# Pacing the table scatters and interleaving the end of attention in an attention-plus-experts kernel

## The chip, the cores and the metric

The kernel runs on one core of a Trainium2 chip. The metric is the device time of one execution in microseconds (us); the lower the better. Engines are written as in the profile: PE is TensorE (matmuls), PEld its weight loads, DVE is VectorE, ACT is ScalarE, POOL is GpSimd, SP is SyncE, which here only issues DMAs. L432 is line 432 of the kernel before.

## The reference

Pooled attention, and then a mixture of experts of which each token uses one or none:

```
k_p = k.reshape(B, H, Sp, 8, D).mean(axis=3); v_p likewise      # B=8, H=8, S=576, D=64, Sp=72
attn = softmax(q @ k_p^T / sqrt(D));  x = attn @ v_p             # x: 4608 tokens x 512
do_compute = x @ w_skip > 0                                      # the other tokens keep x
logits = x[do_compute] @ w_gate                                  # 8 experts
e = argmax(logits);  gate = softmax(logits)[e]
out = x + gate * (relu(x @ w1[e]) @ w2[e])                       # w1: 512x1024, w2: 1024x512
```

## The kernel before, in words

**Two phases.** The attention works through 36 tiles of 128 tokens in a software pipeline written out by hand (`for t in range(NT)`, L637): in iteration t, PE computes the scores of tile t (L305), DVE finds each head's extreme (`largest`, L312), ACT takes exponentials of tile t-1 (L319), PE transposes tile t-2 (L330, L334), multiplies tile t-4 with the pooled values (L348, L350), and DVE normalises tile t-5 (L365 to L372) and SP stores it to `out`. So x of tile i is made in iteration i + 5, and "tile 32" below means iteration t = 32. The order on PE, ACT and DVE is that of the program text; the order on POOL and SP is the framework's, which puts an instruction where its own estimate has it ready, and which adds the waits that the data needs, by program order.

**Routing.** The tokens' gate logits come out of the value matmul (`l8`). After each of six groups of tiles (`GROUPS = [9, 9, 7, 6, 3, 2]`) `route` works in small DVE steps (L393 to L429), an exp on ACT (L409) and rank matmuls on PE (L413, L415): logits minus the largest (l, which stands in PSUM), the chosen expert, the token's rank in it. That gives `di`, each token's row in a table in DRAM (token number and gate, by expert), and `scatter(j)` (L431) writes the rows of one tile with an indirect DMA from POOL. `pending` holds the scatters not yet issued; each iteration issues up to `SCATTERS` of them (L709). A dropped token has a row number out of bounds and isn't written.

**Near tokens.** After the second group (18 tiles) the first 256 tokens of the first expert are known. `near_tokens` registers two callbacks: `ids` (L457) `NIDS` iterations later reads rows 0 to 255 of the table into SBUF, `gathers` (L461) `NWAIT` iterations later computes their slots on DVE (L462) and gathers their x into `ring[:, 3]` and `ring[:, 4]` (L464). In the last two iterations PE transposes them (`tx`, L492, copied by ACT L494 and subtracted by DVE L495), and after the loop the first expert's two layers for these tokens are computed in 16 steps (`l1`, `l2`: L502 to L504, L517 to L519) beside the last routing and the planning of the expert loop (`slots`). Their results (L523) go back with an indirect store, that of the first 128 at once (L525), that of the second in the loop's POOL stream (L1016). Meanwhile the first unit's tokens are gathered into `ring[:, 0:3]` (L889), and `tx` transposes these too (`follow`, L788), when two steps are left.

**The expert loop.** One block with a stream per engine follows (`experts`). Units of up to three tiles of one expert's tokens are transposed, multiplied (L1088 to L1090, L1103 to L1106), scattered (L1007) and the next ones gathered (L1002), with weights loaded one expert ahead. Every matmul is split in high and low halves, three products for one.

Also on POOL: the sums over pooled values (`pool_v`, L240 to L247, then L282 and L285, which PE needs at each change of batch) and the low halves of the first expert's weights (L560).

Of the kernel before, what the change touches and what calls it, by code (L numbers as in the profile page):

```python
# [26 lines left out]
F32 = mybir.dt.float32  # L27
# [39 lines left out]
WROWS = 4.0  # L67
LEAD = 0.5
NLAST = 2
TWO = 1  # L70
QUARTERS = 288, 320, 352, 384
HALF = 64
BIT = 3
SCATTERS = 3
NIDS = 4
NWAIT = 5
WARM = 3
SLOTS = 3 * (MAXU + 2)
NO_TOKEN = 1 << 20
# [82 lines left out]
def attention(tc, nc, q, k, vm, vr, cf, w1, w2, whi, wlo, out, c, pay, offs, table, load_constants, near, bufs, late, early, fin):  # L162
    with ExitStack() as ctx:
# [27 lines left out]

        side_ps = ps_m.tile([128, 512], F32, name="mps")
        scratch = side_ps[:, 512 - GMAX * 20:]

        def load_k(b, part=0):
            n = 4 * SP * POOL
# [112 lines left out]
        def largest(sc, nm):  # L309

            for i in range(2):
                nc.vector.tensor_reduce(nm[:, i * 4:i * 4 + 4], sc[i].rearrange("p (h k) -> p h k", k=SP),  # L312
                                        axis=AX.X, op=ALU.min)
            yield

        def exped(sc, nm):
# [56 lines left out]
            nc.sync.dma_start(out[t * 128:(t + 1) * 128, :], flat(x))  # L373
            yield

        scatters, pending = [], []
        starts = [sum(GROUPS[:i]) for i in range(len(GROUPS))]

        def route(t0, n):


            last = t0 + n == NT
            m = n if last else GMAX
            room = ap.tile([128, n * 20], F32, name="r_room", bufs=1) if last else scratch
            lp = room[:, 0:n * 9].rearrange("p (j e) -> p j e", e=9)
            l, skip = lp[:, :, 0:NE], lp[:, :, NE]
            r8 = eq = room[:, m * 9:m * 9 + n * NE].rearrange("p (j e) -> p j e", e=NE)
            cm, se, ds = (room[:, m * (17 + i):m * (17 + i) + n] for i in range(3))
            bc = lambda x: x.unsqueeze(2).broadcast_to([128, n, NE])
            new = lambda name, *s, dt=F32: ap.tile([128, GMAX] + list(s), dt, name=name)[:, :n]  # L390
            mx = new("r_mx"); no = new("r_no"); cn = new("r_cn"); oh = new("r_oh", NE, dt=BF16)
            ex = new("r_ex", NE); sn = new("r_sn"); di = new("r_di", dt=I32)
            nc.vector.tensor_reduce(lp, l8s.pop(t0)[:, :n].rearrange("p j h c -> p j c h"), axis=AX.X, op=ALU.add)  # L393
            yield
            nc.vector.tensor_reduce(mx, l, axis=AX.X, op=ALU.max)
            yield
            nc.vector.tensor_scalar(no, skip, 0.0, float(NO_TOKEN), ALU.is_le, ALU.mult)
            yield
            nc.vector.tensor_tensor(l, l, bc(mx), ALU.subtract)
            yield  # L400
            nc.vector.scalar_tensor_tensor(eq, l, 0.0, epos.unsqueeze(1).broadcast_to([128, n, NE]), ALU.is_equal, ALU.mult)
            yield
            nc.vector.tensor_reduce(cm, eq, axis=AX.X, op=ALU.max)
            yield
            nc.vector.tensor_tensor(cn, cm, no, ALU.add)
            yield
            nc.vector.tensor_tensor(oh, eq, bc(cn), ALU.is_equal)
            yield NEXT
            nc.scalar.activation(ex, l, AF.Exp)  # L409

            rk = side_ps[:, 0:(n + 1) * NE].rearrange("p (j e) -> p j e", e=NE)
            for j in range(n):
                nc.tensor.matmul(rk[:, j:], c["ones"], oh[:, j].unsqueeze(1).broadcast_to([128, n + 1 - j, NE]),  # L413
                                 start=(j == 0), stop=False)
            nc.tensor.matmul(rk[:, 0:n], c["lower"], oh, start=False, stop=True)  # L415
            nc.vector.tensor_tensor(r8, rk[:, 0:n], offs.unsqueeze(1).broadcast_to([128, n, NE]), ALU.add)
            nc.vector.tensor_tensor(offs, offs, rk[:, n], ALU.add)
            yield NEXT
            nc.vector.tensor_tensor(r8, r8, oh, ALU.mult)
            yield  # L420
            nc.vector.tensor_reduce(se, ex, axis=AX.X, op=ALU.add)
            yield
            nc.vector.tensor_reduce(ds, r8, axis=AX.X, op=ALU.add)
            yield
            nc.vector.tensor_scalar(sn, se, 1e-9, None, ALU.add)
            yield
            nc.vector.tensor_tensor(di, ds, no, ALU.add)
            yield
            nc.vector.reciprocal(pay[:, t0:t0 + n, 1], sn)  # L429

            def scatter(j):  # L431
                m = nc.gpsimd.indirect_dma_start(table, bass.IndirectOffsetOnAxis(ap=di[:, j:j + 1], axis=0),  # L432
                                                 pay[:, t0 + j, :], None, bounds_check=NE * NTOK - 1, oob_is_err=False)
                for other in scatters:
                    tc.declare_no_dep(m.ins, other, reason="rows of the table are written once")
                scatters.append(m.ins)

            pending.extend(lambda j=j: scatter(j) for j in range(n))
            if t0 + n == EARLY:
                yield from near_tokens()  # L440

        def near_tokens():

            count = offs[:, 0:1]
            less = ap.tile([128, 1], F32, name="less")
            nn = ap.tile([128, 1], F32, name="nn")
            nc.vector.tensor_scalar(nn, count, 256.0, 2.0, ALU.is_ge, ALU.mult)
            yield
            nc.vector.tensor_scalar(less, count, 256.0, float(NO_TOKEN), ALU.is_lt, ALU.mult)
            yield  # L450
            nc.vector.tensor_scalar(near["first"][:, 0:1], nn, 128.0, None, ALU.mult)
            yield
            nc.vector.tensor_scalar(near["jt"][:, 0:1], nn, -1.0, float(JT), ALU.mult, ALU.add)
            yield
            nc.vector.tensor_tensor(near["place"], c["place"], nn, ALU.add)

            def ids():  # L457
                assert not pending
                nc.sync.dma_start(near["ids"], table[0:256, 0:2].rearrange("(s l) t -> l s t", l=128))

            def gathers():  # L461
                nc.vector.tensor_scalar(near["slot"], near["ids"][:, :, 0], less, None, ALU.add)  # L462
                for i in range(2):
                    nc.gpsimd.indirect_dma_start(bufs["ring"][:, 3 + i, 0:D], None, out[0:EARLY * 128],  # L464
                                                 bass.IndirectOffsetOnAxis(ap=near["slot"][:, i:i + 1], axis=0),
                                                 bounds_check=EARLY * 128 - 1, oob_is_err=False)
            later[t + NIDS] = ids
            later[t + NWAIT] = gathers
            yield
# [3 lines left out]
        def tile_steps():  # L473
# [40 lines left out]
            def l2(i, part):  # L514
# [6 lines left out]
                def result():  # L521
                    res = bufs["ring"][:, 3 + i, 0:D]
                    nc.vector.scalar_tensor_tensor(res, ps, near["ids"][:, i, 1:2], res, ALU.mult, ALU.add)  # L523
                    if i == 0:
                        nc.gpsimd.indirect_dma_start(out, bass.IndirectOffsetOnAxis(ap=near["slot"][:, 0:1], axis=0),  # L525
                                                     res, None, bounds_check=NTOK - 1, oob_is_err=False)
                return result if part == 3 else None

            got = [lambda f2=f2, part=part: l1(f2, part) for f2 in range(4) for part in range(2)]
# [107 lines left out]
        for t in range(NT):  # L637
# [60 lines left out]
                vt[1] = load_v(1)  # L698
            if t == 1:
                start_k(2)  # L700
            if t in (FILL, FILL + 4):
                n = (NE * NTOK + 128) * RT // 128 // 17
                nc.gpsimd.memset(init[:, 0:n], NO_TOKEN if t == FILL else 0.0)
# [2 lines left out]
                                      init[:, 0:n].unsqueeze(1).broadcast_to([128, 17, n]))  # L706
            if t >= WSTART:
                next(wgen, None)
            for _ in range(min(SCATTERS, len(pending))):  # L709
                pending.pop(0)()  # L710
            later.pop(t, lambda: None)()
            if t == NT - 4:
                load_weights(range(5))
# [26 lines left out]

        def products(n):

            while steps and len(waiting) < 3 and clock["pe"] < clock["dve"] + n:
                while 4 < len(steps) <= 8 and len(waiting) >= len(steps) - 4:
                    evacuate()
                after = steps.pop(0)()
# [30 lines left out]
        for wait in slots(tc, nc, c, offs, table, near, bufs, out, fin, ap, ps_m):  # L777
            if wait:

                end = clock["dve"] + wait  # L780
                while clock["pe"] < end and steps:
                    clock["dve"] = max(clock["dve"], clock["pe"] - 2.0)
                    products(2.5)
                    evacuations(clock["pe"] - 1.0)
                clock["dve"] = max(clock["dve"], end)
            else:
                side(STEP)
        follow = [lambda: [tx(ring[:, i], i)() for i in range(3)]]  # L788
        assert not routes.gens
        held = [kinds(e, fin["nti"]) for e in (nc.tensor, nc.scalar, nc.vector)]  # L790
        while steps or waiting or follow:
            clock["dve"] = max(clock["dve"], clock["pe"] - 2.0)
            products(2.5)
            if waiting:
                evacuate()
            if follow and len(steps) <= NLAST:
                follow.pop()()
        return held


# [106 lines left out]
def experts(tc, nc, out, w1, w2, whi, wlo, slot, gate, nti, held, near, bufs, ident, psum):  # L907
# [4 lines left out]
    with tc.tile_critical():  # L912
# [67 lines left out]
        with nc.Block(no_gpsimd_drain=True) as blk:  # L980
# [10 lines left out]
            def _(g):  # L991
# [21 lines left out]
                        done(f"gat{i}", 16)  # L1013
                        V(g, f"land{i}")

                scatter(near["slot"][:, 1:2], 4)  # L1016
                gather(3)
                gather(5)
                done("sc1", 16)
                gather(4)  # L1020
                landed()
                more, on = g.alloc_register("more"), g.alloc_register("on")
                g.reg_load(more, nti[0:1, 2 * UNITS:2 * UNITS + 1])
# [267 lines left out]
```

## Time and profile before

| | |
|---|---|
| time, median of 3 runs | 568.61 us (568.09 to 570.25) |
| the profiled execution | 568.01 us, its span 566.2 us |
| mean granted TensorE clock | 0.967 |
| PE / DVE / ACT / POOL busy | 91% / 52% / 43% / 38% of the span |
| attention with its routing, up to PE's first expert matmul | 0 to 220.4 us |
| expert loop | 220.4 to 566.2 us |

Busy time counts instructions that an engine executes. Text in brackets at the end of a timeline row is the engine's idle time just before that instruction and what, by the semaphores, ended it; "issue" means nothing that the profile shows. [...]

### The profile page before, as it was taken

To read this page: it belongs to the slowest core of one execution; us is meant where nothing else is said; L and a number is where in the kernel's file an instruction comes from. 1 tells how busy PE (TensorE), PEld (TensorE's weight loads), DVE (VectorE), ACT (ScalarE), POOL (GpSimd) and SP (SyncE) were. 2 spreads that over 40 slices of the span, in tenths; PEclk is the share of its full clock that TensorE was granted. 3 is DMA by queue.
4 is the path that set the end of the run, shared out by engine and by line. 5 is a ranking of instruction groups with operands and counts; after the bars stand their busy time and mean duration, and the time that the engine had idled before them with its cause. 6 is when DMAs were issued, how large, how long until landed. Compare 5 with 4: busy or idle time off the path is not lost. (4 is left out here: it accounts for less than half of the span.)

```text
span 566.2 us, 10990 instructions
## 1 busy us (share of the span) xinstructions
PE 517.2 (91%) x3346; PEld 466.1 (82%) x3347; DVE 294.6 (52%) x697; ACT 244.9 (43%) x671; POOL 217.3 (38%) x294
## 2 busy tenths in 40 slices
PE   5899986987878887989999999999999999999994
PEld 2799775776767776888889888989989899989893
DVE  4476746866637542235353545222364648465653
ACT  4598766887852101114232333111243436344441
POOL 5754556299842424130333034223242024304042
PEclk9699997999989788999999999999999999999998
DMA  8999894785651121012451325201144537572210
GB/s 294 380 340 370 335 353 159 278 287 175 201 204 66 41 76 37 22 51 75 158 180 45 113 110 182 74 19 53 56 156 151 198 117 256 197 246 75 101 45 7
DMA packets 35799, 88.92 MB, mean 157 GB/s; under 512 B 7213, under 2 KB 9961, under 8 KB 33887
## 3 DMA queue, kind: packets, MB, share of 16 engines
q1 hardware_dynamic: 27648, 73.98, 37.2%
q0 software_dynamic: 8112, 14.47, 7.8%
q8 instruction: 18, 0.29, 0.2%
q14 instruction: 21, 0.17, 0.1%
HBM read 74.37 MB, written 22.85 MB: 172 GB/s over the span
## 5 line engine op out<-in xcount | busy, mean ns | idle before, releaser
L1088 PE MATMUL psl<-xhi,w1hi 128*128 128x256 f32 (+3 forms) x416 | 123.4, 297 | 5.2 <-PEq L918 3.7
L1090 PE MATMUL psl<-xhi,w1lo 128*128 128x256 f32 (+3 forms) x416 | 122.9, 295 | 0.0
L1089 PE MATMUL psl<-xlo,w1hi 128*128 128x256 f32 (+3 forms) x416 | 122.8, 295 | 0.0
L1144 ACT ACTIVATE hhi<-psl 128x256 fp32r<-128x256 f32 (+4 forms) x104 | 41.9, 403 | 157.5 <-ACTq L918 156.1
L1007 POOL DMA_INDIRECT out<-ring,slot x39 | 39.8, 1019 | 178.4 <-POOLq L918 144.4
L1103 PE MATMUL psf<-w2hi,hhi 128*128 128x512 f32 x240 | 94.8, 395 | 0.9 <-PEq L918 0.9
L1104 PE MATMUL psf<-w2lo,hhi 128*128 128x512 f32 x240 | 93.6, 390 | 0.6 <-issue 0.6
L1201 DVE SCALAR_TENSOR_TENSOR hlo<-psl,hhi 128x256 fp32r<-128x256 f32 (+2 forms) x104 | 43.8, 423 | 82.2 <-DVEq L918 77.7
L1088 PEld LDWEIGHTS psl<-xhi,w1hi 128*128 128x128 f32 x416 | 79.8, 192 | 7.0 <-issue 6.5
L1089 PEld LDWEIGHTS psl<-xlo,w1hi 128*128 128x128 f32 x416 | 79.8, 192 | 0.4
L1090 PEld LDWEIGHTS psl<-xhi,w1lo 128*128 128x128 f32 x416 | 79.8, 192 | 0.0
L1106 PE MATMUL psf<-w2hi,hlo 128*128 128x512 f32 x200 | 78.0, 390 | 0.0
L319 ACT ACTIVATE e<-sc,nm 128x72 f32<-128x72 f32 x288 | 65.1, 343 | 4.1 <-DVE nm L312 3.6
L348 PE MATMUL o<-blocks,pT 128*128 128x148 f32 (+1 forms) x304 | 49.9, 301 | 11.1 <-DVE x L372 6.9
L1190 DVE SCALAR_TENSOR_TENSOR ring<-psf,ring 128x512 f32 x25 | 18.7, 750 | 74.2 <-DVEq L918 74.2
L1103 PEld LDWEIGHTS psf<-w2hi,hhi 128*128 128x128 f32 x240 | 45.1, 188 | 9.8 <-issue 1.1
L348 PEld LDWEIGHTS o<-blocks,pT 128*128 128x128 f32 (+1 forms) x304 | 41.2, 184 | 13.8 <-issue 6.4
L1104 PEld LDWEIGHTS psf<-w2lo,hhi 128*128 128x128 f32 x240 | 45.1, 188 | 8.6
L1002 POOL DMA_INDIRECT ring<-out,slot x39 | 44.3, 1135 | 15.2 <-issue 12.4
L312 DVE TENSOR_REDUCE nm<-sc 128x4 f32<-128x288 f32 x72 | 32.2, 453 | 32.1 <-PE sc L305 15.7
L1153 ACT ACTIVATE xhi<-psd 128x512 fp32r<-128x512 f32 x36 | 18.9, 599 | 67.0 <-ACTq L918 67.0
L432 POOL DMA_INDIRECT table<-pay,r_di x36 | 35.4, 984 | 27.5 <-DVE rc L367 12.1
(219 smaller groups left out, 878.6 us busy)
## 6 DMA issues: line engine op xcount, KB each, us to landing
stage<-in_w SPq DMA_DIRECT2D x64, 512.0 KB, 4.0
out<-x SPq DMA_DIRECT2D x36, 256.0 KB
stage<-in_k SPq DMA_DIRECT2D x6, 1152.0 KB
hlo<-in_vm SPq DMA_DIRECT2D x4, 1024.0 KB
hhi<-in_vm SPq DMA_DIRECT2D x4, 1024.0 KB
xlo<-in_q SPq DMA_DIRECT2D x6, 512.0 KB
qt<-in_q SPq DMA_DIRECT2D x6, 512.0 KB
xhi<-in_q SPq DMA_DIRECT2D x5, 512.0 KB
```

The costliest lines, as they stand in the source:

```text
L319: nc.scalar.activation(e[:, h, :], sc[h // 4][:, h % 4 * SP:(h % 4 + 1) * SP], AF.Exp, bias=nm[:, h:h + 1], scale=-1.0)
L348: nc.tensor.matmul(o_[sl, g * 2 * VA:(g + 1) * 2 * VA], pT[:, 2 * a + g, sl], vbd[b % 3][:, 2 * a + g, :], start=(g == 0), stop=False)
L1002: g.indirect_dma_start(ring[:, s % 6, 0:D], None, out, bass.IndirectOffsetOnAxis(ap=slot[:, s:s + 1], axis=0), bounds_check=NTOK - 1, oob_ ...
L1007: g.indirect_dma_start(out, bass.IndirectOffsetOnAxis(ap=offsets, axis=0), ring[:, s % 6, 0:D], None, bounds_check=NTOK - 1, oob_is_err=Fa ...
L1088: t.matmul(ps, whi[0][:, k, w], xhi[:, k, xs], start=(k == 0), stop=False)
L1089: t.matmul(ps, whi[0][:, k, w], xlo[:, k, xs], start=False, stop=False)
L1090: last = t.matmul(ps, wlo[0][:, k, w], xhi[:, k, xs], start=False, stop=(k == 3))
L1103: t.matmul(ps, hhi[:, k, sl], whi[1][:, k, :], start=(k == 0), stop=False)
L1104: last = t.matmul(ps, hhi[:, k, sl], wlo[1][:, k, :], start=False, stop=(short and k == 7))
L1106: last = t.matmul(ps, hlo[:, k, sl], whi[1][:, k, :], start=False, stop=(k == 7))
L1144: a.activation(hhi[:, f, xs], psL[f % 3][:, xs], AF.Relu).then_inc(sem["act"], 1)
L1201: m = v.scalar_tensor_tensor(to[:, f], psL[f % 3][:, cs], 0.0, hhi[:, f, cs].bitcast(F32), ALU.max, ALU.subtract)
```

## The change

- Scatters are issued one per iteration up to iteration 21 (`EARLY + LAG`), two per iteration from there (`SCATTERS` 3 to 2); the first one of an iteration also waits for that iteration's second L312 (`turn`). Those issued after the loop don't wait.
- `NIDS` goes from 4 to 6 and `NWAIT` from 5 to 7, and `ids` asks only that 18 scatters have been issued, not that none is pending.
- `route` writes l to a tile in SBUF and reads the experts' places from a copy in PSUM (`places`); `l` and `ex` have one buffer.
- The last two `l2` steps are kept back, and the first unit's three transposes alternate with them; four matmuls without use (`IDLE`) follow the last transposes.
- The indirect store of the first 128 near tokens moves from L525 into the expert loop's POOL stream, ahead of the gathers.

```
-SCATTERS = 3
-NIDS = 4
-NWAIT = 5
+SCATTERS = 2
+NIDS = 6
+NWAIT = 7
+IDLE = 4
...
+        places = side_ps[:, 512 - GMAX * 20 - NE:512 - GMAX * 20]
...
             for i in range(2):
-                nc.vector.tensor_reduce(nm[:, i * 4:i * 4 + 4], ...)
+                m = nc.vector.tensor_reduce(nm[:, i * 4:i * 4 + 4], ...)
+            turn[0] = m.ins
...
-            nc.vector.tensor_tensor(l, l, bc(mx), ALU.subtract)
+            nc.vector.tensor_tensor(l, lp[:, :, 0:NE], bc(mx), ALU.subtract)
-            nc.vector.scalar_tensor_tensor(eq, l, 0.0, epos.unsqueeze(1)..., ALU.is_equal, ALU.mult)
+            nc.vector.scalar_tensor_tensor(eq, l, 0.0, places.unsqueeze(1)..., ALU.is_equal, ALU.mult)
...
-            def scatter(j):
+            def scatter(j, apart=False):
...
+                if apart:
+                    tc.add_manual_dep(m.ins, turn[0].name, ..., reason="a token tile's turn")
-            pending.extend(lambda j=j: scatter(j) for j in range(n))
+            pending.extend(lambda *a, j=j: scatter(j, *a) for j in range(n))
...
-                assert not pending
+                assert len(scatters) >= EARLY
...
-                    if i == 0:
-                        nc.gpsimd.indirect_dma_start(out, ...near["slot"][:, 0:1]..., res, ...)
...
+            if t == START:
+                nc.vector.tensor_copy(places, epos)
...
-            for _ in range(min(SCATTERS, len(pending))):
-                pending.pop(0)()
+            for i in range(min(1 if t < EARLY + LAG else SCATTERS, len(pending))):
+                pending.pop(0)(i == 0)
...
-            while steps and len(waiting) < 3 and clock["pe"] < clock["dve"] + n:
+            while len(steps) > NLAST and len(waiting) < 3 and clock["pe"] < clock["dve"] + n:
...
-        follow = [lambda: [tx(ring[:, i], i)() for i in range(3)]]
-        while steps or waiting or follow:
+        while len(steps) > NLAST:
             clock["dve"] = max(clock["dve"], clock["pe"] - 2.0)
             products(2.5)
             if waiting:
                 evacuate()
-            if follow and len(steps) <= NLAST:
-                follow.pop()()
+        for i in range(3):
+            low = tx(ring[:, i], i)
+            if i == 2:
+                o = ps_o.tile([128, 2, 512], F32, name="o")
+                for _ in range(IDLE):
+                    nc.tensor.matmul(o[:, 0, :], whi[0][:, 0, 0:128], whi[1][:, 0, :], start=True, stop=True)
+            while waiting:
+                evacuate()
+            low()
+            if steps:
+                after = steps.pop(0)()
+                if after:
+                    waiting.append((0.0, after))
...
-                scatter(near["slot"][:, 1:2], 4)
-                gather(3)
+                for i in range(2):
+                    scatter(near["slot"][:, i:i + 1], 3 + i)
                 gather(5)
-                done("sc1", 16)
-                gather(4)
+                for i in range(2):
+                    done(f"sc{i}", 16)
+                    gather(3 + i)
```

## Rows read from the trace of the kernel before

**Rows 1.** The page, part 1: busy time, share of the span, instructions of PE.

```profile
PE 517.2 (91%) x3346; PEld 466.1 (82%) x3347; DVE 294.6 (52%) x697; ACT 244.9 (43%) x671; POOL 217.3 (38%) x294
```

**Rows 2.** Windows: length, busy PE, PEld, DVE, ACT, POOL (instructions), clock, DMA share, GB/s.

```profile
80.00:95.00 15.00, 8.02 (x46) 7.06 (x45) 6.93 (x17) 6.41 (x23) 13.02 (x16) 0.78 0.46 173
95.00:120.00 25.00, 23.10 (x188) 20.87 (x188) 21.06 (x59) 20.96 (x77) 10.75 (x14) 1.00 0.79 284
125.00:135.00 10.00, 5.93 (x44) 5.13 (x43) 4.38 (x13) 5.89 (x21) 8.12 (x8) 1.00 0.43 153
160.00:170.00 10.00, 6.73 (x41) 5.91 (x42) 3.58 (x10) 5.73 (x20) 3.40 (x5) 0.83 0.46 155
150.00:155.00 5.00, 5.00 (x43) 4.99 (x42) 4.17 (x17) 4.28 (x18) 4.20 (x5) 1.00 1.01 343
...
220.00:225.00 5.00, 4.64 (x26) 4.66 (x27) 0.42 (x1) 0.39 (x1) 4.00 (x7) 0.66 0.21 57
```

**Rows 3.** Timeline of POOL (start, us, line, operation): scatters, and a gather.

```profile
75.57 1.18 POOL L432 DMA_INDIRECT table<-pay,r_di  x1 [0.65 <-DVE rs L365]
...
86.00 0.97 POOL L432 DMA_INDIRECT table<-pay,r_di  x1 [0.30 <-issue]
...
122.57 1.02 POOL L432 DMA_INDIRECT table<-pay,r_di  x1 [0.16 <-DVE nm L312]
...
150.86 1.08 POOL L464 DMA_INDIRECT ring<-out,nslot  x1 [0.30 <-DVE nslot L462]
...
154.73 1.03 POOL L432 DMA_INDIRECT table<-pay,r_di  x1 [0.17 <-DVE l L371]
...
178.73 1.01 POOL L432 DMA_INDIRECT table<-pay,r_di  x1 [12.10 <-DVE rc L367]
```

**Rows 4.** Timelines of DVE, ACT and PE beside the first and the fourth run.

```profile
81.33 0.17 DVE L365 TENSOR_SCALAR rs<-o 128x8 f32<-128x8 f32 x1 [4.03 <-PE sc L305]
...
85.60 0.60 ACT L331 ACTIVATE pT<-pt 128x512 f32<-128x512 f32 x1 [5.47 <-PE sc L305]
...
189.39 0.28 PE L503 MATMUL sc<-xlo,w1hi 128*128 128x256 f32 x1 [0.33 <-issue]
190.10 0.38 PE L504 MATMUL sc<-xhi,w1lo 128*128 128x256 f32 x1 [0.43 <-issue]
...
191.56 0.60 ACT L509 ACTIVATE hhi<-sc 128x512 fp32r<-128x512 f32 x1 [9.88 <-remote]
```

**Rows 5.** Tiles 31 to 35 and the near tokens: timelines, L459's source view, L1007's landing.

```profile
149.46 1.12 DVE L462 TENSOR_SCALAR nslot<-nids,less 128x2 int32<-128x2 f32 x1
...
151.34 0.68 DVE L372 TENSOR_TENSOR x<-o,rc 128x512 f32<-128x512 f32 x1
...
153.81 0.19 DVE L429 RECIPROCAL pay<-r_sn 128x7 f32<-128x7 f32 x1
...
154.55 0.68 DVE L372 TENSOR_TENSOR x<-o,rc 128x512 f32<-128x512 f32 x1
...
167.94 0.68 DVE L372 TENSOR_TENSOR x<-o,rc 128x512 f32<-128x512 f32 x1
...
168.91 0.66 PE L492 MATMUL pt<-cfs,ring 128*128 128x128 f32 x4
...
L459 SPq DMA_DIRECT2D nids<-table x1: 385/385/385, 142.3 to 142.3; - x1
...
DMA to landing us min/median/max: 2.1/2.8/5.6
```

**Rows 6.** Timelines of PE and DVE at the end of the attention phase.

```profile
213.84 0.66 PE L492 MATMUL mps<-cfs,ring 128*128 128x128 f32 x4 [0.97 <-DVE xlo L495]
...
217.27 0.75 DVE L523 SCALAR_TENSOR_TENSOR ring<-sc,nids,ring 128x512 f32<-128x512 f32 x1 [1.41 <-PE sc L519]
...
220.36 0.37 PE L1088 MATMUL psl<-xhi,w1hi 128*128 128x256 f32 x1 [3.13 <-PEq L918]
```

**Rows 7.** Waits of PE, 120 to 150: total us, times, longest.

```profile
PE mps L413 <- ACT r_ex L409: 1.2, 1, 1.2
```

More of the change, by code (lines that the diff above doesn't have):

```diff
@@ L311, in largest @@
             for i in range(2):
-                nc.vector.tensor_reduce(nm[:, i * 4:i * 4 + 4], sc[i].rearrange("p (h k) -> p h k", k=SP),
-                                        axis=AX.X, op=ALU.min)
+                m = nc.vector.tensor_reduce(nm[:, i * 4:i * 4 + 4], sc[i].rearrange("p (h k) -> p h k", k=SP),
+                                            axis=AX.X, op=ALU.min)
+            turn[0] = m.ins
             yield
@@ L374, in normalised @@
             yield
-        scatters, pending = [], []
+        scatters, pending, turn = [], [], [None]
         starts = [sum(GROUPS[:i]) for i in range(len(GROUPS))]
@@ L385, in route @@
             lp = room[:, 0:n * 9].rearrange("p (j e) -> p j e", e=9)
-            l, skip = lp[:, :, 0:NE], lp[:, :, NE]
+            skip = lp[:, :, NE]
             r8 = eq = room[:, m * 9:m * 9 + n * NE].rearrange("p (j e) -> p j e", e=NE)
@@ L389, in route @@
             bc = lambda x: x.unsqueeze(2).broadcast_to([128, n, NE])
-            new = lambda name, *s, dt=F32: ap.tile([128, GMAX] + list(s), dt, name=name)[:, :n]
+            new = lambda name, *s, dt=F32, **kw: ap.tile([128, GMAX] + list(s), dt, name=name, **kw)[:, :n]
             mx = new("r_mx"); no = new("r_no"); cn = new("r_cn"); oh = new("r_oh", NE, dt=BF16)
-            ex = new("r_ex", NE); sn = new("r_sn"); di = new("r_di", dt=I32)
+            l = new("r_l", NE, bufs=1); ex = new("r_ex", NE, bufs=1); sn = new("r_sn"); di = new("r_di", dt=I32)
             nc.vector.tensor_reduce(lp, l8s.pop(t0)[:, :n].rearrange("p j h c -> p j c h"), axis=AX.X, op=ALU.add)
             yield
-            nc.vector.tensor_reduce(mx, l, axis=AX.X, op=ALU.max)
+            nc.vector.tensor_reduce(mx, lp[:, :, 0:NE], axis=AX.X, op=ALU.max)
             yield
@@ L398, in route @@
             yield
-            nc.vector.tensor_tensor(l, l, bc(mx), ALU.subtract)
+            nc.vector.tensor_tensor(l, lp[:, :, 0:NE], bc(mx), ALU.subtract)
             yield
-            nc.vector.scalar_tensor_tensor(eq, l, 0.0, epos.unsqueeze(1).broadcast_to([128, n, NE]), ALU.is_equal, ALU.mult)
+            nc.vector.scalar_tensor_tensor(eq, l, 0.0, places.unsqueeze(1).broadcast_to([128, n, NE]), ALU.is_equal, ALU.mult)
             yield
@@ L436, in scatter @@
                 scatters.append(m.ins)
-            pending.extend(lambda j=j: scatter(j) for j in range(n))
+                if apart:
+                    tc.add_manual_dep(m.ins, turn[0].name, mybir.DependencyInfo(
+                        mybir.DependencyClass.Sync, mybir.DependencyReason.DATA), reason="a token tile's turn")
+            pending.extend(lambda *a, j=j: scatter(j, *a) for j in range(n))
             if t0 + n == EARLY:
@@ L523, in result @@
                     nc.vector.scalar_tensor_tensor(res, ps, near["ids"][:, i, 1:2], res, ALU.mult, ALU.add)
-                    if i == 0:
-                        nc.gpsimd.indirect_dma_start(out, bass.IndirectOffsetOnAxis(ap=near["slot"][:, 0:1], axis=0),
-                                                     res, None, bounds_check=NTOK - 1, oob_is_err=False)
                 return result if part == 3 else None
@@ L780, in attention @@
                 end = clock["dve"] + wait
-                while clock["pe"] < end and steps:
+                while clock["pe"] < end and len(steps) > NLAST:
                     clock["dve"] = max(clock["dve"], clock["pe"] - 2.0)
```

## The prediction

> **What bounds the kernel now.** I read the page first [rows 1]: PE is busy 91% of the span, so time can only be won where PE stands still or runs at its lower clock. The windows view then shows where that is [rows 2]. The expert loop behind 225 us leaves little. The attention part (up to 180 us) has undisturbed stretches such as 95 to 120, where PE is busy 23.10 of 25 us (0.924), and three bad ones: 80 to 95 with 8.02 of 15 us busy at a mean granted clock of 0.78, 125 to 135 with 5.93 of 10, and 160 to 170 with 6.73 of 10 at 0.83. The timeline of POOL [rows 3] shows what these share. Each lies in the second half of, or just behind, a run of table scatters (L432), which POOL issues every 1.3 us without a pause: 9 from 75.57 on (the last at 86.00), 9 from 122.57, 7 from 154.73 and 9 from 178.73. Rows of a group become ready together, POOL has nothing else to do, and so "three per tile" in the program text has become all of them at once.
>
> The timelines of the other engines [rows 4] say what happens there: everything stands still, not one engine. DVE starts L365 at 81.33 after 4.03 us of idleness, ACT starts L331 at 85.60 after 5.47 us although its transposes on PE were long issued, ACT stands 9.88 us before L509 at 191.56, and there PE itself takes 0.71 us from one matmul of 256 columns to the next (189.39 to 190.10), with no wait in the program between them. The fourth run has almost no other DMA traffic beside it and stalls as well, so a full DMA queue is not needed. The first scatters of a run seem to do no harm: ACT's idle time begins at 85.60 - 5.47 = 80.1, four scatters into the run (DVE's at 77.3, but that one may begin as a regular wait for PE). Two gathers of the same kind in a row at 150.86 [rows 3] stand in a window in which PE is busy 5.00 of 5.00 us [rows 2]. So the stall looks like a matter of density, and the change goes at density.
>
> **The change part by part.** All sums are against the profiled execution's 568.01 us (span 566.2); the median of the three runs is 0.6 higher.
>
> *Pacing.* The first group's 9 scatters go one per tile, those of groups two and three two per tile, the first of a tile waiting for that tile's second L312 on DVE. A tile takes 3.21 us undisturbed (151.34 to 154.55) [rows 5], so POOL then issues 1.3 or 2.6 us in it and pauses. What is to be had: in each bad window, work at full clock is busy time times granted clock, and at the undisturbed 0.924 it would take 8.02 x 0.78 / 0.924 = 6.8 us instead of 15 (8.2 won), 5.93 / 0.924 = 6.4 instead of 10 (3.6 won), 6.73 x 0.83 / 0.924 = 6.0 instead of 10 (4.0 won). Sum 15.8 us [rows 2]. Bounds: 0, if the stall belongs to each scatter however it stands, and 15.8. I take 15.8, by the nearest row, the harmless pair at 150.86. The fourth run (groups four to six, behind the loop) is not paced: there the scatters are issued without the wait, and its stall stays.
>
> *What waits behind the new wait.* POOL is in order; a scatter that waits for a tile's L312 holds back what stands behind it, the value sums (L240 to L242), the low weight halves (L560) and the products L282 and L285 that PE needs at a change of batch. Value sums had been done early. Each change of batch can find POOL one scatter (1.3 us) late; three such changes lie in the paced stretch, some slack covers part: cost 1.0 us, bounds 0 and 4.
>
> *The near tokens' chain* is where I expect a loss. The read of the first 256 table rows (L459) moves from 4 to 6 tiles behind group two, the gathers from 5 to 7. Group two's last route step is in tile 26, so the read comes in tile 32, and group three's rows become ready in that same tile (L429 at 153.81, while the next tile's x is at 154.55) [rows 5]. In the text two of its scatters are issued ahead of the read. They write the table, the read reads it, so it waits for both. Before, the read was issued at 142.3, with all 18 scatters done and group three's not begun [rows 5]. From E = 153.81: POOL issues the first scatter 0.9 us later (154.73) [rows 3], the second 1.3 on, E + 2.2. Landing of an indirect store is 2.1, 2.8 or 5.6 us (min, median, max of L1007's row) [rows 5]. I use it for each hop: second scatter landed E + 5.0, read landed E + 7.8, DVE's L462 to POOL's gather 1.4 us (149.46 to 150.86) [rows 3, 5], gather landed E + 12.0. PE wants it for the transposes L492 in tile 34: x of that tile at 154.55 + 3.21, and 0.97 us on as in tile 35 (167.94 to 168.91) [rows 5], E + 4.9. PE, in order, would stand 7.1 us; with the fastest landings 5.0, with the slowest 15.5. Below that it could be nothing, if the tiles around it are slower than 3.21 us. I take 7.1: the DMA share in 150 to 155 is 1.01 [rows 2], which speaks against the minimum, and the maximum would have to strike three times. Before, this slack was two tiles longer, so the stall is new.
>
> [...]
>
> *Logits on chip.* l goes to its own SBUF tile, a copy of epos into PSUM (one DVE instruction, 0.2 us, in tile 5, hidden beside PE). The rank matmuls L413 no longer share a bank's tile with what ACT's exp L409 reads: 1.2 us of PE's wait for r_ex in 120 to 150 goes [rows 7]. The DVE steps keep their size; nothing else moves.
>
> *The end.* Before, three transposes of the first unit stand in a row and the third waits 0.97 us for DVE (213.84), then two l2 steps, DVE's L523 from 217.27 to 218.02, PE's first expert matmul at 220.36 after 3.13 us idle [rows 6]. After, transposes and steps alternate, which hides the 0.97; but behind the last transposes now stand ACT's copy (0.60, as L331 of the same size [rows 4]) and DVE's subtraction (0.68, as L372 [rows 5]) where L523 (0.75) stood: 0.97 - (0.60 + 0.68 - 0.75) = 0.4 us. The four idle matmuls (0.28 us or more each [rows 4]) lie in a gap in which PE waits anyway. In 220 to 225 PE runs at a granted clock of 0.66 [rows 2], which costs 5 x 0.34 = 1.7 us; a shorter gap may or may not keep the clock, so I count half, 0.8. Bounds of both together 0 and 2.1; taken 1.2. The early store that moves into the loops (L525) was off the path, and the gather of slot 3 comes one scatter later, 1.3 us, with most of a unit in hand: 0.
>
> **Sum.** 15.8 + 1.2 + 1.2 - 7.1 - 1.0 = 10.1; 568.0 - 10.1 = 557.9, and 0.6 for the median: **558.5 us**.
>
> **The rivals.**
> (a) *The chain is hidden.* If landings are quick or the tiles around 32 to 34 slower than 3.21 us, the 7.1 is not paid: 551.4 us. For it: route steps make some tiles longer. Against it: the read is ordered behind scatters that become ready in its own tile.
> (b) *The pacing does not spread.* It is done by a wait, and a POOL that is behind (eight instructions of value sums in a row) finds the waits passed and issues several tiles' scatters together again. Only the first group's stretch would be won, 3.6 + 4.0 lost again: 566.1 us.
> (c) *Nothing happens*: neither stall nor chain moves, the end and L413 give 2.4: 566.2 us.
> (d) *Slower.* The stall is a price of each scatter, 15.8 / 25 = 0.63 us wherever it stands. Then pacing returns nothing and the chain is paid: 568.6 - 2.4 + 7.1 + 1.0 = 574.3 us. It becomes slower than before as soon as less than 5.7 / 15.8, some 36%, of the stall comes back. For it: DVE's idle time begins early in its run [rows 4]. Against it: the harmless first scatters. [...]
>
> **How the numbers follow.** Forecast 0.45 (its own range 554 to 563), (a) 0.22, (b) 0.13, (c) 0.07, (d) 0.13. The range from 550.0 to 568.5 takes in (a) to (c) and leaves out (d) and the best of (a). A measurement of this kernel can tell 0.5% (2.8 us) from no change; (b) lies about on that line and is halved. Faster 0.73, same 0.14, slower 0.13.
>
> **What would show it.** Right: single scatters some 3.5 us apart from 75 us on, then pairs; no idle time of 4 us or more on ACT and DVE before the loop's end; x of tile 28 some 12 us earlier; the stall before L509 still there; PE idle for several us before its first L492, released by a gather. Wrong: stalls of DVE and ACT beside single scatters (d), runs of four or more scatters (b), L492 without a wait (a), or a PE that waits for POOL's L282.

## The result, and the profile after

The change makes the kernel slower: median 574.32 us (573.13 to 575.14) against 568.99 us for the kernel before, ratio 1.0073, 95% interval 1.0049 to 1.0098. The forecast was 558.5. The profiled execution took 573.13 us, its span 571.3.

Where x of a token tile is made (start of DVE's L372, now L375) tells where the time goes; us from the start of the span:

| tile | before | after | difference |
|---|---|---|---|
| 12 | 75.79 | 75.52 | -0.27 |
| 15 | 95.57 | 86.84 | -8.73 |
| 20 | 117.42 | 117.03 | -0.38 |
| 23 | 133.19 | 132.06 | -1.13 |
| 28 | 154.55 | 153.97 | -0.58 |
| 30 | 167.94 | 174.53 | +6.58 |
| 33 | 185.44 | 191.62 | +6.19 |
| first expert matmul | 220.36 | 226.51 | +6.15 |
| end of the span | 566.2 | 571.3 | +5.1 |

8.7 us are won by tile 15 and lost again by tile 20; another 7.2 are lost between tiles 28 and 30. The windows of after show the places (columns as in [rows 2]; the clock is the granted share of the full one, in these rows between 0.50 and 1.00):

```profile
80.00:95.00 15.00, 12.16 (x96) 11.46 (x95) 14.23 (x30) 12.47 (x44) 10.08 (x14) 1.00 0.89 329
...
105.00:115.00 10.00, 5.13 (x39) 4.58 (x38) 9.24 (x13) 4.29 (x18) 9.69 (x13) 0.86 0.28 90
...
125.00:130.00 5.00, 2.98 (x23) 2.58 (x21) 1.66 (x5) 0.73 (x4) 4.08 (x5) 1.00 0.58 219
130.00:135.00 5.00, 3.24 (x16) 3.00 (x17) 3.68 (x9) 4.66 (x17) 3.02 (x4) 0.78 0.68 227
...
160.00:165.00 5.00, 0.00 (x0) 0.00 (x0) 2.06 (x7) 0.40 (x2) 2.99 (x3) 0.85 0.88 266
165.00:170.00 5.00, 0.09 (x1) 0.12 (x2) 0.00 (x0) 0.00 (x0) 3.58 (x5) 0.50 0.74 263
```

The first stretch is largely healed (PE 12.16 of 15 us at full clock, where it was 8.02 at 0.78). New is a hole in 105 to 115, in which PE is busy only 5.13 of 10 us while DVE and POOL are both busy almost throughout. The second stretch, 125 to 135, is as bad as before. In 160 to 170 PE does next to nothing.

**The hole at 105**, called the collision below. Timelines of DVE and POOL of after:

```profile
89.45 3.51 DVE L562 TENSOR_TENSOR w1lo<-stage,w1hi 128x512 fp32r<-128x512 f32 x1
95.45 0.68 DVE L562 TENSOR_TENSOR w1lo<-stage,w1hi 128x512 fp32r<-128x512 f32 x1
105.28 6.22 DVE L562 TENSOR_TENSOR w1lo<-stage,w1hi 128x512 fp32r<-128x512 f32 x2
...
106.29 2.76 POOL L242 TENSOR_TENSOR hlo<-hlo 128x256 f32<-128x256 f32 x4
109.02 0.71 POOL L242 TENSOR_TENSOR vl<-vl 64x256 f32<-64x256 f32 x1
109.70 1.25 POOL L243 TENSOR_TENSOR hlo<-hlo 128x512 f32<-128x512 f32 x1
110.92 0.89 POOL L243 TENSOR_TENSOR vl<-vl 64x128 f32<-64x128 f32 x1
```

L562 makes a low half of a weight from two inputs. Where no value sums run beside it, it takes 0.68 to 0.72 us here; beside POOL's value sums (L242 to L244) one takes 3.51 us and another, from 105.92 on the second of the two in the row of 6.22, takes 5.58, while POOL's row of four sums keeps its time (2.76 us, 0.69 each). DVE's steps for x and for the routing stand behind it, and PE behind those (waits of PE, after):

```profile
PE mps L267 <- DVE offs L420: 4.9, 1, 4.9
PE o L351 <- DVE x L375: 4.8, 5, 2.0
```

In the kernel before the same two engines met at the same work and shared it:

```profile
111.04 3.68 POOL L240 TENSOR_TENSOR hlo<-hlo 128x256 f32<-128x256 f32 x4
111.36 2.09 DVE L558 TENSOR_TENSOR w1lo<-stage,w1hi 128x512 fp32r<-128x512 f32 x2
```

**The standstill at 160.** Timelines of POOL, SP, DVE and PE of after:

```profile
153.92 1.01 POOL L435 DMA_INDIRECT table<-pay,r_di  x1 [0.15 <-DVE rc L370]
155.23 0.97 POOL L435 DMA_INDIRECT table<-pay,r_di  x1 [0.30 <-issue]
158.87 0.38 SPq L466 DMA_DIRECT2D nids<-table  x1
160.54 0.23 DVE L469 TENSOR_SCALAR nslot<-nids,less 128x2 int32<-128x2 f32 x1 [4.47 <-DMA nids<-table]
161.29 0.97 POOL L435 DMA_INDIRECT table<-pay,r_di  x1 [5.09 <-DVE rc L370]
162.56 0.98 POOL L435 DMA_INDIRECT table<-pay,r_di  x1 [0.31 <-issue]
163.84 1.04 POOL L471 DMA_INDIRECT ring<-out,nslot  x1 [0.30 <-issue]
169.91 1.09 PE L499 MATMUL pt<-cfs,ring 128*128 128x128 f32 x4 [10.39 <-DMA ring<-out,nslot]
```

This is the chain of the near tokens, link by link: two scatters, the read (L466) behind them, DVE's L469, two more scatters, the gather, PE.

**The second run of scatters** is still one, timeline of POOL: six from 121.70 on, 1.3 us apart.

```profile
121.70 1.02 POOL L435 DMA_INDIRECT table<-pay,r_di  x1 [0.16 <-DVE x L375]
123.02 0.97 POOL L435 DMA_INDIRECT table<-pay,r_di  x1 [0.30 <-issue]
...
128.12 0.98 POOL L435 DMA_INDIRECT table<-pay,r_di  x1 [0.30 <-issue]
131.18 0.99 POOL L435 DMA_INDIRECT table<-pay,r_di  x1 [0.79 <-DVE nm L314]
```

Only the first scatter of an iteration has the wait. By the semaphores of these instructions the second to the fifth of the six are the four of this group that don't wait for DVE: the framework, free in the order on POOL, put them in a row, ahead of the waiting ones.

### The profile page after: what moved, and what is told of

Its sections match the earlier page's. It is cut to its first block, busy times and chain, and to the rows that moved or that the text cites. A ratio compares the mean times of both kernels' runs of the same rounds, so it can differ in the third digit from the quotient of the medians.

```text
span 571.3 us, 11007 instructions
## 1 busy us (share of the span) xinstructions
PE 516.7 (90%) x3350; PEld 466.9 (82%) x3351; DVE 300.1 (53%) x698; ACT 244.9 (43%) x671; POOL 217.0 (38%) x294
## 5 line engine op out<-in xcount | busy, mean ns | idle before, releaser
L351 PE MATMUL o<-blocks,pT 128*128 128x148 f32 (+1 forms) x304 | 51.5, 307 | 6.5 <-DVE x L375 4.8
L351 PEld LDWEIGHTS o<-blocks,pT 128*128 128x128 f32 (+1 forms) x304 | 43.0, 191 | 9.0 <-issue 4.2
```

The source lines that it names most:

```text
L351: nc.tensor.matmul(o_[sl, g * 2 * VA:(g + 1) * 2 * VA], pT[:, 2 * a + g, sl], vbd[b % 3][:, 2 * a + g, :], start=(g == 0), stop=False)
```

## The experiments

They ran in four lots, each lot on a chip of its own, with the kernel before beside it. In the first and the last lot the kernel before took 570.9 and 570.2 us, in the second and third 547.9 and 547.7. That was not looked for, and it turned out to be the main finding; so every ratio here is to the kernel before on the same chip. A chip that stalls is one on which the kernel before takes about 570 us and stands still beside its runs of scatters; lot two shows the other kind. "The changed kernel" is the one with the change. It ran again in lot three alone. In lot one it is taken at its 1.0073, measured on the prediction's chip, which stalls too, and 1% is taken as 5.7 us.

### Lot one (the kernel before 570.9 us)

**The early read in the changed kernel.**

```
-NIDS = 6
-NWAIT = 7
+NIDS = 4
+NWAIT = 5
```

> The changed kernel with the table read and the gathers back at 4 and 5 tiles behind group two; all else stays. Theory (the chain: the read stands behind two scatters of group three, and PE waited 10.4 us before L499 for the gather): the read is issued before group three's scatters, that wait falls under 1 us, and the 7.2 us that x lost between tiles 28 and 30 come back: about 567 us. Rival (the read only decides which scatters stand in a row): with the read out of the way group three's scatters run together, a stall as in the third run of before comes back (4 us), and the time is about 571 us. Second rival (the wait before L499 covers something else that is late, such as DVE or ACT): no change, 574 us.

Measured 564.87 us, ratio 0.9911 (0.9880 to 0.9943), 1.6% or 9.2 us below the changed kernel. The gathers are issued at 148.99 and 150.36, ahead of group three's scatters, and PE meets a landed gather:

```profile
159.34 0.65 PE L499 MATMUL pt<-cfs,ring 128*128 128x128 f32 x4 [1.31 <-issue]
```

The chain is the cause of the standstill at 160. It costs more than the 7.2 us net of the table, since in the kernel before a stall of its own lay in that place: from tile 28 to tile 30 the kernel before takes 13.4 us, the changed kernel 20.6, and with the early read it is 11.1 here and 8.1 where nothing stalls (lot three).

**The wait on every scatter, in the changed kernel.**

```
-                pending.pop(0)(i == 0)
+                pending.pop(0)(True)
```

> The changed kernel, but each scatter in the loop waits for its tile's L314, not the first of a tile's two alone. Theory (density: a row of scatters harms, single ones and pairs do not): group two's scatters stand in pairs 3.2 us apart instead of six in a row from 121.7 us, the stall in 125 to 135 (PE busy 2.98 and 3.24 of 5 us) goes, and x is about 3.6 us earlier by tile 26; the chain of the late read stays, so 571 us. Rival (a price of each scatter, 0.63 us wherever it stands): the idle time only moves, 574 us. Second rival (POOL held back by more waits): PE waits for L284 or L287 and the time is above 575 us.

Measured 570.07 us, ratio 1.0005 (0.9973 to 1.0037), 0.7% or 3.9 us below the changed kernel. PE in 125 to 130 goes from 2.98 to 4.53 of 5 us, and tile 23 comes at 127.84 (132.06 in the changed kernel). The same nine scatters, in twos and threes with 1.5 us between (a low half on POOL), stall hardly anything there, PE being busy 9.53 us of 125 to 135: a price of each scatter is out.

**The late read alone, in the kernel before.**

```
-NIDS = 4
-NWAIT = 5
+NIDS = 6
+NWAIT = 7
...
-                assert not pending
+                assert len(scatters) >= EARLY
```

> The kernel before with the table read 6 and the gathers 7 tiles behind group two, nothing else. Theory (the chain costs by itself, whatever the pacing): the read stands behind scatters of group three, PE waits before L492 for the gather, and the time is 6 to 8 us above the kernel before: 575 to 577 us. Rival (the chain is late only because pacing makes tiles 28 to 34 come earlier against it): under 2 us above, at most 571 us.

Measured 576.90 us, ratio 1.0146 (1.0092 to 1.0200), 8.3 us slower. The chain needs no pacing. Waits of PE, and a row of POOL's timeline, a scatter behind the read:

```profile
PE pt L492 <- DMA ring<-out,nslot: 8.4, 1, 8.4
```

```profile
165.94 0.97 POOL L432 DMA_INDIRECT table<-pay,r_di  x1 [3.65 <-DMA nids<-table]
```

**No low halves on DVE, in the changed kernel.**

```
-WPOOL = 3
+WPOOL = 0
```

> The changed kernel with all low halves of the first expert's weights on POOL (the first three chunks' six were on DVE, L562). Theory (collision: DVE's L562, which took 3.51 and 6.22 us beside POOL's value sums instead of 0.68, hold back DVE and so PE): x keeps the 8.7 us that the first group's pacing has won at tile 15, PE's 4.9 us before L267 and 2.0 us before L351 go, about 566 us. Rival (POOL's added 7.5 us of work makes the value sums late instead): PE waits for L284 or L287, 572 to 578 us. Second rival (the slow instructions lie in DVE's idle time, and the gain is lost by something else): 574 us.

Measured 565.71 us, ratio 0.9927 (0.9899 to 0.9956), 1.5% or 8.3 us below the changed kernel. Tile 20 comes at 108.17 instead of 117.03. The collision theory holds, and the first rival is there in part: POOL has become late for PE, by 3.5 us before 139.73.

```profile
PE pt L499 <- DMA ring<-out,nslot: 9.5, 1, 9.5
PE o L351 <- POOL blocks L284: 5.6, 3, 3.5
```

### Lot two (the kernel before 547.9 us)

**The three edits together, in the changed kernel** (early read, wait on every scatter, `WPOOL = 0`).

> The changed kernel with three edits at once: table read and gathers back at 4 and 5 tiles, every scatter in the loop waits for its tile, all low halves of the first expert's weights on POOL. Theory (three separate losses, chain 9.2 us, second run 3.9 us, collision 8.3 us, each by its own run's ratio against the changed kernel's): they add, ratio 0.970, about 552 us. Rival (POOL becomes the bound: with the low halves on POOL PE already waited 5.6 us for L284): 3 to 6 us of that don't come, 555 to 558 us, and PE waits for L284 near 140 us.

Measured 550.31 us: the forecast time, but ratio 1.0051 (1.0031 to 1.0072), since here the kernel before takes 23 us less than in lot one. Both expectations had the wrong premise.

**The same with `WPOOL = 1`.**

> As the three edits at once, but the first chunk's two low halves stay on DVE, which in the changed kernel ran beside scatters in 0.68 us each; so POOL has 2.5 us less. Theory (only DVE's low halves beside POOL's value sums do harm): no L562 over 0.8 us, and the time is that of the three edits or up to 2 us less, 550 to 552 us. Rival (any low half on DVE is caught, since POOL's order shifts): an L562 of 3 us or more again, and 4 us more than the three edits.

Measured 552.17 us, ratio 1.0074 (1.0046 to 1.0101): no gain over the three edits. The two low halves on DVE took 0.68 and 1.53 us, the longer one beside a low half on POOL. That is neither the rival's 3 us nor the theory's under 0.8.

**No low halves on DVE, in the kernel before.**

> The kernel before with all low halves of the first expert's weights on POOL, nothing else. Theory (the low halves on DVE cost only where POOL's value sums keep them out; in the kernel before they took 0.68 to 1.22 us): no gain, 568 to 571 us, slower if POOL's added 7.5 us come in the way of L282. Rival (six instructions fewer on DVE help by themselves, which would explain the 8.3 us of the same edit in the changed kernel): 561 to 564 us.

Measured 551.58 us, ratio 1.0056 (1.0032 to 1.0081): a loss of 3 us here, where in the changed kernel of lot one the same edit won 8.3. The two stand on chips of different kinds, so this alone doesn't show the collision to be new with the change; that the low halves on DVE never take over 1.22 us without the pacing, on either kind (the kernel before; lot two, with the new end), does. The loss comes with waits of PE for POOL, 5.7 us in all:

```profile
PE o L348 <- POOL blocks L282: 5.7, 2, 3.1
```

**The new end alone, in the kernel before** (`products`, the loops behind it and the store as in the change's diff).

> The kernel before with the new end alone: transposes of the first unit alternate with the last two steps, four idle matmuls, the store of the first near tokens in the loop. Prediction's step: 1.2 us less, 567.8 us (0.4 from the interleaving, 0.8 from the clock). Theory by the trace of the changed kernel, where the stretch from tile 33's x to the first expert matmul took 34.89 us against 34.92 and the expert loop 344.8 against 345.8: the gain is 1.0 us and all of it is the clock behind the first expert matmul (1.00 instead of 0.66). Rival: it moves nothing or costs up to 2 us, since the indirect store now stands ahead of the gathers: 569 to 571 us.

Measured 548.56 us, ratio 1.0000 (0.9981 to 1.0018): nothing, at most 1.0 us either way. Its trace, and the one before, show where this chip is faster. Windows of the kernel before with the new end; the scatters of its first run stand at 75.88, 77.36 and so on to 86.37, as in [rows 3]:

```profile
75.00:80.00 5.00, 5.00 (x50) 4.65 (x49) 3.36 (x14) 4.96 (x20) 3.43 (x5) 1.00 0.89 313
80.00:85.00 5.00, 5.00 (x42) 4.89 (x41) 4.73 (x12) 5.00 (x19) 3.87 (x4) 1.00 1.02 382
85.00:90.00 5.00, 5.00 (x41) 4.77 (x41) 4.34 (x11) 4.77 (x20) 4.60 (x6) 1.00 0.94 290
```

Nine scatters in a row, 1.28 us apart, and PE is busy throughout. Where it stalls, with the same scatters (the kernel before on the prediction's chip, same windows):

```profile
75.00:80.00 5.00, 5.00 (x51) 4.65 (x50) 2.23 (x9) 4.96 (x19) 3.52 (x4) 1.00 0.96 329
80.00:85.00 5.00, 2.84 (x22) 2.44 (x20) 1.66 (x5) 0.13 (x1) 3.78 (x5) 1.00 1.01 383
85.00:90.00 5.00, 1.82 (x10) 1.24 (x10) 1.55 (x3) 3.29 (x12) 4.68 (x7) 0.83 0.20 71
```

So the stall that pacing is to heal is not there in every lot. No chip served in two lots; that the chip makes the difference, and not something else that changed from lot to lot, is likely and not shown.

### Lot three (the kernel before 547.7 us, no stall)

**The changed kernel again.**

> The changed kernel itself once more, beside the kernel before on the same chip. Theory (the stall beside rows of scatters belongs to the chip: on the chip of the first four experiments the kernel before takes 571 us and stalls, on that of the second four 548 us and doesn't, with the same scatters at the same times): where the kernel before takes about 570 us, this takes 574; where it takes about 548, pacing has nothing to win and the collision (some 8 us) and the chain (some 7 us) are paid in full, 560 to 564 us, ratio 1.022 to 1.03. Rival (the two chips differ by an even scale, 570 to 548, and the stall only shows more on one): ratio 1.007 on either.

Measured 565.07 us, ratio 1.0322 (1.0296 to 1.0349): no even scale; the change costs 17.4 us where there is no stall to heal. Both losses stand there undiluted: x takes 30.1 us from tile 15 to tile 20 where the kernel before with the new end takes 21.7 (lot two), 8.5 us for the collision, and 18.6 us from tile 28 to tile 30 where it takes 8.1. A row of DVE's timeline and two windows:

```profile
104.21 6.21 DVE L562 TENSOR_TENSOR w1lo<-stage,w1hi 128x512 fp32r<-128x512 f32 x2
```

```profile
105.00:110.00 5.00, 1.04 (x17) 0.80 (x15) 5.00 (x1) 0.91 (x3) 4.98 (x8) 1.00 0.01 1
...
160.00:165.00 5.00, 0.00 (x0) 0.00 (x0) 0.00 (x0) 0.00 (x0) 3.78 (x5) 0.50 1.04 388
```

**The early read again.**

> The changed kernel with the table read and gathers back at 4 and 5 tiles, once more. Theory: 7 to 9 us less than the changed kernel on either chip, since the chain has nothing to do with the stall: about 565 us where the kernel before takes 570, about 555 where it takes 548. Rival (the chain was long only because landings are late on a chip that stalls): on a chip without the stall no gain over the changed kernel.

Measured 554.33 us, ratio 1.0111 (1.0083 to 1.0139), 10.7 us below the changed kernel. The chain has nothing to do with the stall.

**The three edits again.**

> The three edits together once more (early read, every scatter waits, all low halves on POOL). Theory (on a chip that stalls the three losses add): ratio 0.970, about 552 us where the kernel before takes 570; on a chip without the stall 1.005 again, 550 us. Rival (POOL is the bound near 140 us on either chip): 555 to 558 us where the kernel before takes 570.

Measured 550.61 us, ratio 1.0033 (1.0010 to 1.0055). What is left of the cost is, by the waits, POOL: PE waits 7.9 us in three places for L284, 5.65 of them once, up to 140.69 us; with the new end alone (lot two) such waits were 2.2.

**Pacing alone, in the kernel before.**

```
-SCATTERS = 3
+SCATTERS = 2
...
+            turn[0] = m.ins
...
+                if apart:
+                    tc.add_manual_dep(m.ins, turn[0].name, ...)
...
-            for _ in range(min(SCATTERS, len(pending))):
-                pending.pop(0)()
+            for i in range(min(1 if t < EARLY + LAG else SCATTERS, len(pending))):
+                pending.pop(0)(True)
```

> The kernel before with the pacing alone, every scatter in the loop waiting for its tile's L312: no late read, no new end, logits as before. Theory (pacing wins what stalls there are, and brings DVE's low halves L558 beside POOL's value sums where they are kept out): where the kernel before takes 570 us, 15.8 - 8.3 = 7.5 less, about 562 us; where it takes 548, the collision alone, 554 to 557 us, and an L558 of 3 us or more. Rival (the collision comes from another part of the change): 554 us where the kernel before takes 570, 548 us where it takes 548, all L558 under 1.3 us.

Measured 554.39 us, ratio 1.0125 (1.0087 to 1.0163), 6.7 us slower. The collision belongs to the pacing (timeline of DVE; L563 is the low half in this kernel):

```profile
103.31 6.16 DVE L563 TENSOR_TENSOR w1lo<-stage,w1hi 128x512 fp32r<-128x512 f32 x2
```

### Lot four (the kernel before 570.2 us, stalls)

**The three edits a third time.**

> The three edits together (early read, every scatter waits, all low halves on POOL), for a chip on which the kernel before takes about 570 us. Theory (the three losses add there): ratio 0.970, about 552 us, the same absolute time as on the chips without a stall (550.3 and 550.6), since spread scatters leave nothing to stall but the run behind the loop. Rival (what stalls is also spread scatters, in part): 556 us or more. Where the kernel before takes 548 it tells nothing new: 550.5.

Measured 553.63 us, ratio 0.9717 (0.9670 to 0.9764). The losses add, and with them gone the change wins 16.1 us on a chip that stalls, where the prediction had 15.8 for the pacing. A run of four scatters, from 148.34 to 152.25, still stalls here: PE is busy 4.06 us of 150 to 155, and 5.00 in lot three.

**The three edits, the last batch's large sums on DVE.**

```
-            for x, y, eng in ((vt, vs, nc.gpsimd if b else nc.vector), (vl, ls, nc.gpsimd)):
+            for x, y, eng in ((vt, vs, nc.gpsimd if 0 < b < B - 1 else nc.vector), (vl, ls, nc.gpsimd)):
```

> The three edits, and of the last batch's value sums the large ones (4.8 us on POOL) on DVE. Theory (POOL is the bound there: PE waits 5.7 us for L284 near 135 us): that wait falls to 1 us or less and the time to 546 to 548 us on a chip where the three edits take 550.5. Rival (DVE, in order, then holds back its own steps and so x, or is kept out again beside POOL's low halves): no gain, 550 us or more, and PE waits for DVE instead.

Measured 554.46 us, ratio 0.9719 (0.9680 to 0.9758): no gain. The waits of PE for POOL shrink from 7.5 to 2.8 us, but the first row, 0.3 us with the three edits, takes their place, as the rival said:

```profile
PE mps L276 <- DVE l L374: 4.2, 1, 4.2
PE o L351 <- POOL blocks L284: 2.8, 2, 1.8
```

**Pacing alone again.**

> The kernel before with the pacing alone, for a chip on which the kernel before takes about 570 us. Theory: pacing wins the stall, 15.8 us, and pays the collision, 6.7 us by its run without a stall: 561 us; and it lies 9 to 11 us above the three edits. Rival (the price of each scatter): 576 us. Where the kernel before takes 548 it tells nothing new: 554.4.

Measured 560.64 us, ratio 0.9842 (0.9804 to 0.9880). The time is as expected; the three edits lie 7.0 us below it, less than the 9 to 11 expected. Pacing alone wins 9.0 us here and loses 6.7 in lot three. The low halves beside the value sums take the same in both (3.41 us, and 6.2 for two), so the 15.7 us between the two are, by that, what it takes of the stall.

The fastest version on a chip that stalls is the one with the three edits, 2.8% below the kernel before; the sums on DVE change nothing. On a chip that doesn't stall nothing tried is faster than the kernel before.

## Why the prediction was wrong, step by step

**What bounds the kernel** was read rightly for the chip of that trace: runs of six to nine scatters stall PE, DVE and ACT [rows 3, 4] (busy 2.84, 1.66 and 0.13 us of 80 to 85 before; beside the six from 121.70, 2.98, 1.66 and 0.73 us of 125 to 130 after), one of four stalls less (PE 4.06 of 5 us, lot four), and pairs and threes hardly do (PE 9.53 of 10 us, the wait on every scatter). Density was the right word, by the wait on every scatter and by pacing alone. That the stall is not the kernel's alone, a trace of one chip could not show.

**Pacing, +15.8.** The size was right for pacing that spreads: with the wait on every scatter it takes 15.7 us of the stall (lots three and four). In the change the first group's 8.2 came (8.7 by tile 15; its first three scatters, 75.30 to 78.06, still stand in a row, with PE busy 9.12 us of 75 to 85, where it was 7.84). The second group's 3.6 did not: six scatters still in a row; with the wait on all of them 3.9 us came. The third group's 4.0 can't be seen by itself, because PE stood for the gather there. The text of the change had "the first one of an iteration also waits", and the step took it to hold the second too; on POOL, whose order the framework sets, the four without a wait went ahead of the waiting ones. Rival (b) had the outcome for one group, with another reason; (a) and (c) fell with the gather's 10.39 us.

**The missing term: DVE's low halves, 8.3 us** (no low halves on DVE, lot one; 8.5 by the tiles of lot three; pacing alone, with all its costs, lost 6.7 there). The step on what waits behind the new wait named the value sums, and asked who waits for them. It did not ask beside what they now run. This is where the forecast failed: the 8.7 us of the first group were spent on it (-8.73 at tile 15, -0.38 at tile 20). Rival (d) hung a price on the scatters wherever they stand; but beside a scatter, at 95.45 and 105.28, an L562 took 0.68 and 0.72 us, and it was the sums that held it up.

**The chain, -7.1.** Right in kind and place, too small: 8.3 us by itself (lot one), 9.2 and 10.7 in the changed kernel. Read to DVE was quicker than assumed (158.87 to 160.54, 1.7 for 2.8 us). But L469 to gather was 3.3 us for 1.4, since two scatters of the next iteration stand ahead of the gathers on POOL and wait for the read too (the row of the late read alone shows it), and from the gather to PE it was 6.1 for 2.8.

**POOL late, -1.0 (0 to 4).** In the changed kernel PE does not wait for L284 where the chip stalls; without the stall it does, 3.8 us (lot three), where the kernel before with the new end has 2.2 and pacing alone 2.4. So the step was inside its bounds, by 0.2 to 1.6 us of waits. The 7.5 to 7.9 us of the three edits do not measure it: low halves moved to POOL give 5.7 us of such waits in the kernel before, without any pacing.

**L413, +1.2.** Not shown, and no run has this step alone. The wait for r_ex has gone, and one for DVE stands at the line now (waits of PE, after):

```profile
PE mps L416 <- DVE mps L404: 1.3, 1, 1.3
```

The kernel before with the new end waited 2.8 us for r_ex, in two places, so the waits at this line did shrink. But in lot three x takes 76.4 us from tile 12 to tile 28 in pacing alone, with the old logits, and as much in the changed kernel with the early read.

**The end, +1.2.** Not shown: from x of tile 33 to the first expert matmul it took 34.92 us before and 34.89 after; the loop behind is 1.0 us shorter, in this trace; the end by itself gave 1.0000.

The measured sum by the table: -8.7 + 8.3 - 0.2 + 7.2 - 0.4 - 1.0 = +5.2, rounded, against +5.1 of the span. Against the forecast, 15.8 us are missing. The collision (8.3), the second run (3.9), a chain longer by 2.1 (9.2 for 7.1) and the 1.2 each of L413 and the end, less the 1.0 for POOL that was not paid, make 15.7; these come from separate runs, so that it fits so well is partly luck. That 574.3 is also the figure of rival (d) is chance: its mechanism, a price of each scatter, fell in lot one.

## What to carry to other kernels

When an edit moves work on one engine in time, list not only who waits for that work but what now runs beside it on other engines: here a low half of 0.68 us on DVE took up to 5.58 beside POOL's sums. A wait that is to spread a row of instructions must stand on every one of them: on the first of each iteration alone, it left six scatters in a row. And before a stall that shows in one trace is made the reason of a change, look for it on a second chip: here the same pacing changes the time by -1.6% on one and by +1.3% on another.

## What the runs showed of the hardware

**A stall that came on some chips only.** On the chips of lots one and four, and of the prediction's trace, PE, DVE and ACT stand still beside runs of scatters (in the prediction's trace PE is busy 2.84, DVE 1.66 and ACT 0.13 us of 80 to 85) and the kernel before takes 569 to 571 us; on the chips of lots two and three they don't (5.00, 4.73 and 5.00 us, the kernel before with the new end), and it takes 548. The first run of scatters is issued at the same times within 0.4 us (kernel before, and with the new end). The traces differ in one more thing. On the chips that stall, semaphore events of DMAs are missing: the trace of before holds 618 of them in 0 to 60 us and 28 in 80 to 90; that of the kernel before with all low halves on POOL (lot two) 605 and 205. The row on the scatters in the page of the profile shows it as a landing time that can't be given (before, and the kernel before with the new end):

```profile
table<-pay,r_di POOLq DMA_INDIRECT x36
```

```profile
table<-pay,r_di POOLq DMA_INDIRECT x36, 4.1
```

Missing records do not always go with a stall: with the three edits, 120 to 130 us holds 46 such events in lot four and 189 in lot two, and PE is busy 9.36 and 9.51 of the 10 us. Whether the stall and the missing events have one cause, or one leads to the other, is open, and no run here can tell it.

**DVE shut out for several instructions.** Beside POOL's value sums, one behind the other, L562 took 3.51 us, and of the next two, 6.22 us together, the second took 5.58; on a chip without the stall it was 3.41 and 6.21 (lot three). In the kernel before, beside the same sums, the two engines took turns (L558 0.83 to 1.22 us each, POOL's four pieces 3.68 instead of 2.76). In the changed kernel five POOL instructions ended between 106.3 and 110.9 while one L562 was held up. What decides between taking turns and being shut out was not found.
